# Attention and two feed-forward layers on one core: raw weight words fetched later and rescaled on two engines, and two sum groups moved into the last layer

## The chip, the cores and the metric

The kernel runs on one core of a Trainium2 chip. The metric is the device time of one execution in microseconds; the median of several executions counts. Engines are named as the profile names them: PE (TensorE; PEld are its weight loads), DVE (VectorE), ACT (ScalarE), POOL (GpSimd) and SP (SyncE, which here only issues DMAs; SPq is its queue).

## The reference

```python
def _attn_ref(q, k, v, M_prev, z_prev, beta):        # B, H, S, D = 4, 8, 576, 64
    scores = scale * np.matmul(q, k.transpose(0, 1, 3, 2))      # causal mask, softmax -> a
    local = np.matmul(a, v)
    q_p = phi(q)
    mem_out = einsum('bhsd,bhde->bhse', q_p, M_prev) / (einsum('bhsd,bhd->bhs', q_p, z_prev) + 1e-06)
    return g * mem_out + (1 - g) * local                        # g = sigmoid(beta), per head
def _moe_ref(x, w_in, w_out):                        # 2304 tokens, 512 -> 2048 -> 512
    h = x @ w_in
    return (h * np.cos(h)) @ w_out
def _moe2_ref(x, w_in, w_out):
    h = x @ w_in
    return (h * np.tanh(softplus(h))) @ w_out
reference = _moe2_ref(_moe_ref(_attn_ref(...)))
```

The four weight matrices come in as float64 and reach the chip as pairs of 32-bit words; the kernel turns each pair into float32 itself.

## The kernel before

**Stages.** The attention runs over 16 pairs of heads with five steps each (`stage_a`: scores, mask, exp and the row's weighting; `stage_b`: transposes; `stage_c`: the output). The first feed-forward layer is computed in two halves of its 2048 hidden units. The first half (`seq1`, 256 tokens at a time) is woven into the attention from about 120 us on and ends at about 480 us; the second half (`seq2`, 512 tokens at a time) runs from there to about 670 us. The last layer (`strassen_ffn`) does its products with seven sums of blocks in place of eight blocks, in 24 groups of about 14.5 us.

**Raw words.** `fetch` loads 512 KB of raw word pairs into one of four `wst` buffers from SP's queue, and `to_f32` makes float32 of them in four steps: the high word is rescaled (`scaled(kind, ...)`, line 134 on POOL, line 130 on ACT), ACT makes a float of the low word (line 145), and DVE joins the two (lines 146 and 147). For the first layer, `load_half` then splits the result into two parts (`wh`: lines 130 and 134; line 183 subtracts on POOL and DVE in turn); 16 pieces for each half. `TURNS` is a table that says which engine takes each kind of step: `"p"` POOL, `"a"` ACT, `"v"` DVE, several letters in turn.

**Sum groups.** The last layer's weights are 16 pieces (`strassen_pieces`: eight of `w_in`, eight of `w_out`). `strassen_weights` takes two raw loads for each, forms four sums (line 561, POOL), splits seven blocks in four lots (lines 130 and 567) and stores each lot to DRAM (lines 570 and 573, SP's queue), from where `load_w` (line 625) fetches them in the last layer. It is a generator: each `next` is one small step. Six pieces (`gi`) are made during the attention, ten (`gc`) during the second half.

**Order.** A scheduler sets the order on each engine. `tc.issue_after(x)` puts what a block records behind instruction x on x's own engine; it adds no wait for other engines. `marks` holds the latest instruction of a kind: `act` the exp, `vec` the reciprocal of the row sums (line 277), `pool` the weighting of the row (line 279), `sp` the last store of a pair's attention output (line 347).

Of the kernel before, what the change touches and what calls it, by code (L numbers as in the profile page):

```python
# [25 lines left out]
LOAD0 = 9  # L26
AHEAD = 3
SUM0 = 38
SUMS = 6
SUM2 = 2  # L30
XSUM0 = 37
XLOAD0 = 63
CONVR = 0.9
# [4 lines left out]

TURNS = dict(
    sc0="p", aT0="a",  # L40
    sc="p", ws="p", w0l="pv", w1l="vp", w2l="vp", gl="p", gh="v", bh="a", mh="a",
    wh="ap", aT="av", yl="p", ml="p", y0="v", y1="a", aD="v", y3="a", yf="vp", yz="v", mz="vp", x3l="v", x3l0="pv", x3d0="p", x3d="v", ws4="p", ws2="a", wh2="a",
)

# [6 lines left out]
def attention_moe_moe_kernel(  # L51
# [489 lines left out]
                 for tl in range(n)] +  # L541
                [([wo[:, f] for f in (2 * tl, 2 * tl + 1)], "h c f", woD[tl]) for tl in range(n)])

    def strassen_weights(pieces):

        made = []
        raws = ahead([src for srcs, _, _ in pieces for src in srcs])
        for _ in range(AHEAD):
            next(raws)
            yield  # L550
        for _, order, dst in pieces:
            pc = []
            for _ in range(2):
                pc.append(next(raws).rearrange(f"p ({order}) -> p h c f", c=2, h=2))
                yield
            (a11, a21), (a12, a22) = [[q[:, h] for h in range(2)] for q in pc]
            sw = wk.tile([P, 4, 2, P], F32, tag="sw", name="sw", bufs=BUFS["sw"])
            s1, s2, s3, s4 = [sw[:, k] for k in range(4)]
            for i, (d, x, y, op) in enumerate(((s1, a21, a22, ALU.add), (s2, s1, a11, ALU.subtract),
                                               (s3, a11, a21, ALU.subtract), (s4, a12, s2, ALU.subtract))):  # L560
                turn_of("ws4").tensor_tensor(d, x, y, op)
                if i % 2:
                    yield
            for k0, k1, t in ((0, 2, pc[1]), (2, 3, pc[0][:, 0:1]), (3, 5, sw[:, :2]), (5, 7, sw[:, 2:])):
                ws = wk.tile([P, 2, 2, 2, P], F32R, tag="ws", name="ws", bufs=BUFS["ws"])[:, :k1 - k0]
                scaled("wh2", ws[:, :, 0], t)
                turn_of("w2l").tensor_tensor(ws[:, :, 1], t, ws[:, :, 0].bitcast(F32), ALU.subtract)
                made.append((dst[:, k0:k1], ws.rearrange("p k l c f -> p k (l c f)").bitcast(F32)))
                if len(made) > 1:
                    nc.sync.dma_start(*made.pop(0))  # L570
                yield
        for m in made:
            nc.sync.dma_start(*m)

    def strassen_x(t0, out, store=False):

# [63 lines left out]
                es.enter_context(tc.issue_after(marks[e]))  # L640
        return es

    def strassen_ffn(pool, xs, w, fill):

        ng = DFF // (2 * P)
        groups = [(t0, tl) for t0 in range(0, NT, 2 * TS) for tl in range(ng)]
# [5 lines left out]
        stores = []  # L652
        chain = [(k, name) for k in range(0, n, KS) for name in LAST]
        g3 = [wk.tile([P, 2, TS], F32R, tag=f"g3{i}", name="g3", bufs=1) for i in range(BUFS["g3"])]
        sums = [wk.tile([P, TS], F32, tag=f"ac{i}", name="ac", bufs=1) for i in range(14)]
        free = list(range(BUFS["g3"]))

        def bank():
# [109 lines left out]
        for k in range(n + KS):  # L768
# [4 lines left out]
            def product(b, name, first):  # L773
                m = 0
                for c in range(2):
                    for wl, xl in ((0, 0), (0, 1), (1, 0)):
                        nc.tensor.matmul(b, w[name][:, wl, c], x[name][:, xl, c], start=first and m == 0, stop=m == 5,  # L777
                                         skip_group_check=True)
                        m += 1
                if k + 1 < n:  # L780
                    nw[name] = load_w(groups[k + 1][1], name)
                j = PROD.index(name)
                for a in range(STEPS.count((groups[k][1] - ng, j))):
                    with behind():
                        next(coming, None)
# [72 lines left out]
    k_done = 0  # L858
    pieces = [-AHEAD]
    pieces2 = strassen_pieces(w2i, w2o)  # L860
    gi = strassen_weights(pieces2[:SUMS])

    def converted(n):
        while pieces[0] < min(n, 4 * NTL):
# [2 lines left out]

    for kind, s in at:
        if kind == "a" and s >= LOAD0:
            converted(min(s - LOAD0 + 1 - AHEAD, 0))  # L870
        if kind == "a" and s >= CONV0:
            with tc.issue_after(marks["act"]):
                converted(int((s - CONV0 + 1) * CONVR))
        if kind == "a" and s >= SUM0 - AHEAD:
            with tc.issue_after(marks["act"]), tc.issue_after(marks["pool"]), tc.issue_after(marks["vec"]):
                for _ in range(2 if s % 5 == 0 else 1):
                    next(gi, None)
        if kind != "c":
            continue
        b, r = divmod(s, steps_b)  # L880
        if r == steps_b - 1:
            stored[0] = b + 1
        if b == 0:
            continue
        share = (r + 1) / steps_b
        tgt = int(2 * NTL * (b - 1 + (share ** PACE1 if b == 1 else share))) - RES
        while k_done < tgt:
            converted(4 * min(k_done + 2, NTL))
            _, kk = next(m1)
            k_done = max(k_done, kk + 1)  # L890
# [7 lines left out]
                    done_b = next(gb, done_b)  # L898
    b_pools = [psum("psB")]
    drain(gi)  # L900
    gc = strassen_weights(pieces2[SUMS:])
    fill = []
    m2 = ffn(b_pools, seq2, {1: w_b}, elem_cos("bh"), load_block(xsH, xsL, True), mm2_t, fin_full, tail=fill)
    gx = strassen_x(0, {}, True)
# [27 lines left out]
    with tc.issue_after(last_sin[0]):  # L932
        table = nc.scalar.preload_act_table_set("mish").ins
    with tc.issue_after(table), tc.issue_after(marks["xs"]):
        drain(strassen_ffn(b_pools[0], xs, w0, fill))


_OUTS = [((512, 2304), "float32")]
# [62 lines left out]
```

## Time and profile before

| | us |
|---|---|
| median of 3 runs | 1048.62 (1046.93 to 1053.64) |
| the profiled execution's own time | 1047.3 |
| its span, first to last instruction | 1045.5 |
| PE busy in the span | 1006.4 (96%) |
| DVE, ACT, POOL busy | 680.9, 576.8, 625.8 |

PE is busy nearly all the time, so the table is read by its gaps: 39 us of the span in which PE does nothing, and stretches in which its granted clock is below 1.00.

### The profile page before, as it was taken

The numbers are of one execution on the slowest core, as the hardware profiler recorded it, in microseconds if no ns is written. First come the engines' busy times: TensorE is split into PE (matmuls) and PEld (weight loads), VectorE is DVE, ScalarE is ACT, GpSimd is POOL, SyncE is SP. The second block draws the span as 40 slices with busy tenths as digits, with TensorE's granted clock in tenths as the row PEclk, the third lists the DMA queues.
The fourth block names the chain that finished last, engine by engine and source line by source line (L and its number), as shares of the span: only waits on it lengthen the run. The fifth ranks groups of instructions, "written<-read, shape, count | busy, mean of one in ns | idle before, by whom it ended". The sixth has DMA issues, their size and how long they took to land.

```text
span 1045.5 us, 19409 instructions
## 1 busy us (share of the span) xinstructions
PE 1006.4 (96%) x6704; PEld 895.4 (86%) x6704; DVE 680.9 (65%) x1411; ACT 576.8 (55%) x1274; POOL 625.8 (60%) x612
## 2 busy tenths in 40 slices
PE   6988999999999999999999999999999999999996
PEld 3755788787878899998887777999999999999996
DVE  4689865657665545787775877252788347862657
ACT  5886776758575643334565646345453544445441
POOL 3379744455554524655766788355778767786662
PEclk8998999999999999999999999999999999999999
DMA  7477634546442437433788888987987888797882
GB/s 266 136 238 241 208 128 161 180 159 224 151 146 80 145 105 258 151 101 131 264 287 277 327 295 321 402 306 226 321 271 252 276 285 292 235 311 236 276 285 81
DMA packets 121841, 236.19 MB, mean 226 GB/s; under 512 B 11920, under 2 KB 35984, under 8 KB 121744
## 3 DMA queue, kind: packets, MB, share of 16 engines
q1 hardware_dynamic: 121744, 234.95, 66.2%
q8 instruction: 54, 0.88, 0.4%
q14 instruction: 43, 0.35, 0.1%
HBM read 176.44 MB, written 58.46 MB: 225 GB/s over the span
## 4 chain that ended last, share of the span: by engine, by line
PE 76%; DMA 7%; DVE 6%; ACT 3%; POOL 3%; issue 3%; SPq 1%; DVEq 0%; POOLq 0%; ACTq 0%
PE y L494 16%; PE h L777 15%; PE h L428 15%; PE y L748 15%; PE o L339 4%; PE tp L312 3%; PE sp L252 3%; PE o L328 1%; PE mp L292 1%; DMA qd<-in_qT_dram 1%; DMA wst<-in_w1o_dram 1%; DMA xbH<-xsH 1%; POOL at L279 1%; DMA w<-woD 1%; ACT u L387 1%
## 5 line engine op out<-in xcount | busy, mean ns | idle before, releaser
L682 POOL TENSOR_TENSOR g<-us,g 128x384 fp32r<-128x384 f32 x164 | 180.3, 1117 | 99.6 <-ACT g L130 96.3
L494 PE MATMUL y<-g,w 128*128 128x256 f32 (+1 forms) x1344 | 222.8, 318 | 7.1 <-POOL g L400 3.6
L494 PEld LDWEIGHTS y<-g,w 128*128 128x128 f32 x1344 | 191.5, 190 | 35.0 <-issue 10.5
L428 PE MATMUL h<-xbH,w 128*128 128x256 f32 (+1 forms) x896 | 206.5, 317 | 1.3 <-DMA xbH<-xsH 1.3
L748 PE MATMUL y<-g,w 128*128 128x384 f32 x1008 | 195.3, 335 | 3.0 <-DMA w<-woD 2.2
L777 PE MATMUL h<-xc,wq 128*128 128x384 f32 x1008 | 195.5, 334 | 0.0
L748 PEld LDWEIGHTS y<-g,w 128*128 128x128 f32 x1008 | 176.0, 188 | 5.1 <-DMA w<-woD 2.6
L777 PEld LDWEIGHTS h<-xc,wq 128*128 128x128 f32 x1008 | 176.1, 188 | 0.2 <-DVE us L671 0.2
L279 POOL TENSOR_SCALAR at<-at,sm,omg 128x128 f32<-128x128 f32 (+2 forms) x144 | 113.5, 798 | 103.3 <-DVE sm L277 85.8
L400 POOL TENSOR_TENSOR g<-u,g 128x512 fp32r<-128x512 f32 x72 | 103.1, 1449 | 112.5 <-ACT g L130 47.4
L428 PEld LDWEIGHTS h<-xbH,w 128*128 128x128 f32 x896 | 150.9, 191 | 14.4 <-DMA xbH<-xsH 2.1
L428 PE MATMUL h<-xbL,w 128*128 128x256 f32 (+1 forms) x448 | 140.7, 314 | 0.0
L671 DVE TENSOR_TENSOR us<-h,us 128x384 f32<-128x384 f32 x120 | 66.4, 554 | 113.2 <-PE h L777 97.4
L130 ACT ACTIVATE g<-us 128x384 fp32r<-128x384 f32 x168 | 85.7, 523 | 53.9 <-DVE us L666 33.8
L675 ACT ACTIVATE us<-us 128x384 f32<-128x384 f32 x72 | 37.7, 524 | 94.9 <-DVE us L671 94.2
L428 PEld LDWEIGHTS h<-xbL,w 128*128 128x128 f32 x448 | 85.6, 191 | 5.2 <-issue 0.2
L257 ACT ACTIVATE at<-at,mn 128x128 f32<-128x128 f32 (+3 forms) x128 | 70.9, 555 | 25.3 <-DVE mn L254 24.6
L382 ACT ACTIVATE u<-h 128x512 int32<-128x512 f32 x72 | 41.9, 590 | 67.2 <-PE h L428 66.2
L147 DVE SCALAR_TENSOR_TENSOR wst<-wst 128x512 int32<-128x512 int32 x64 | 73.8, 1165 | 0.3
L712 DVE TENSOR_TENSOR ac<-y,ac 128x384 f32<-128x384 f32 x120 | 63.5, 549 | 14.5 <-PE y L748 14.0
L312 PE MATMUL tp<-ident,at 128*128 128x128 f32 x384 | 63.4, 284 | 8.3 <-POOL at L279 5.3
L390 DVE TENSOR_TENSOR u<-h,u 128x512 f32<-128x512 f32 x72 | 46.3, 685 | 36.4 <-ACT u L387 36.4
(106 smaller groups left out, 1538.6 us busy)
## 6 DMA issues: line engine op xcount, KB each, us to landing
wq<-wsD SPq DMA_DIRECT2D x168, 256.0 KB, 3.9
w<-woD SPq DMA_DIRECT2D x168, 256.0 KB, 4.3
wsD<-ws SPq DMA_DIRECT2D x24, 512.0 KB, 3.8
woD<-ws SPq DMA_DIRECT2D x24, 512.0 KB, 5.6
wst<-in_w1i_dram SPq DMA_DIRECT2D x16, 512.0 KB, 4.4
wst<-in_w1o_dram SPq DMA_DIRECT2D x16, 512.0 KB, 4.8
wst<-in_w2i_dram SPq DMA_DIRECT2D x16, 512.0 KB, 4.3
wst<-in_w2o_dram SPq DMA_DIRECT2D x16, 512.0 KB, 5.7
```

The costliest lines, as they stand in the source:

```text
L130: eng.activation(dst, src, AF.Copy, scale=scale)
L147: nc.vector.scalar_tensor_tensor(lo, hi, 3, lo, ALU.logical_shift_left, ALU.bitwise_or)
L257: marks["act"] = nc.scalar.activation(at[:, :N], at[:, :N], AF.Exp, bias=mn[:, j:j + 1], scale=-1.0, accum_out=sm[:, j:j + 1]).ins
L279: marks["pool"] = turn_of("sc", b == 0).tensor_scalar(at[:, :N], at[:, :N], sm[:, j:j + 1], gates[j], ALU.mult, ALU.mult).ins
L312: nc.tensor.transpose(tp[:, c:c + P], at[:, c:c + P], ident)
L400: marks["gl"] = turn_of(kind).tensor_tensor(gL, g, gH.bitcast(F32), ALU.subtract).ins
L428: nc.tensor.matmul(h[:, a * T:(a + 1) * T], w_[:, c, f0:f0 + P], x_[c], start=m == 0, stop=m == 3 * NC - 1)
L494: nc.tensor.matmul(y[e // per][:, cols], w_[:, f, es], g_, start=fst and m == 0 and e % per == 0, stop=lst and m == 2, skip_group_check=True)
L671: marks['v'] = nc.vector.tensor_tensor(c, b, x, ALU.add).ins
L682: ins = turn_of("ml" if k + 1 < n else "mz").tensor_tensor(t[:, 1], x, t[:, 0].bitcast(F32), ALU.subtract).ins
L748: nc.tensor.matmul(y, w_[:, wl, c], x[:, xl], start=m == 0, stop=m == 3 * KS - 1, skip_group_check=True)
L777: nc.tensor.matmul(b, w[name][:, wl, c], x[name][:, xl, c], start=first and m == 0, stop=m == 5, skip_group_check=True)
```

## The change

1. `ws="pa"`: the rescaling of the first layer's raw high words goes to POOL and ACT in turn; it was on POOL alone.
2. The first raw loads (`LOAD0`) are put behind `marks["sp"]`, the first pair's store, on SP's queue. The conversion steps from `CONV0` on are put behind the attention step's exp, its weighting on POOL and its reciprocal on DVE; they were put behind the exp alone.
3. Two of the sixteen pieces (`LATE`, the last two of `w_out`) leave `gc` and are made in the last layer, by `late` steps behind five of the seven products of each group from the second group on. `SUM2` is 5 in place of 2, so that the second half takes 1.2 steps for each unit in place of 1.5.
4. The stores of the pieces in `gc` and of the two late ones are issued from ACT's queue; `gi` stays on SP's.
5. The fourteen accumulators of the last layer are slices of one tile.

```diff
-SUM2 = 2
+SUM2 = 5
+LATE = 2
-    sc="p", ws="p", w0l="pv", ...
+    sc="p", ws="pa", w0l="pv", ...
-    def strassen_weights(pieces):
+    def strassen_weights(pieces, queue):
-                    nc.sync.dma_start(*made.pop(0))
+                    queue.dma_start(*made.pop(0))
-            nc.sync.dma_start(*m)
+            queue.dma_start(*m)
-    def strassen_ffn(pool, xs, w, fill):
+    def strassen_ffn(pool, xs, w, fill, late):
-        sums = [wk.tile([P, TS], F32, tag=f"ac{i}", name="ac", bufs=1) for i in range(14)]
+        sums = wk.tile([P, 14, TS], F32, name="ac")
+        sums = [sums[:, i] for i in range(14)]
...
                 j = PROD.index(name)
+                if k >= 1 and j not in (0, 3):
+                    with behind():
+                        next(late, None)
...
-    gi = strassen_weights(pieces2[:SUMS])
+    gi = strassen_weights(pieces2[:SUMS], nc.sync)
...
         if kind == "a" and s >= LOAD0:
-            converted(min(s - LOAD0 + 1 - AHEAD, 0))
+            with tc.issue_after(marks["sp"]):
+                converted(min(s - LOAD0 + 1 - AHEAD, 0))
         if kind == "a" and s >= CONV0:
-            with tc.issue_after(marks["act"]):
+            with tc.issue_after(marks["act"]), tc.issue_after(marks["pool"]), tc.issue_after(marks["vec"]):
                 converted(int((s - CONV0 + 1) * CONVR))
...
-    gc = strassen_weights(pieces2[SUMS:])
+    gc = strassen_weights(pieces2[SUMS:-LATE], nc.scalar)
+    gd = strassen_weights(pieces2[-LATE:], nc.scalar)
...
-        drain(strassen_ffn(b_pools[0], xs, w0, fill))
+        drain(strassen_ffn(b_pools[0], xs, w0, fill, gd))
```

In the built program, SP's queue begins as follows before the change (`qd`, `kd`, `qt`, `mz` and `vt` are the attention's inputs of a pair, `wst` the raw words):

```order
L220 DMA qd<-in_qT_dram 128x640
L218 DMA kd<-in_kT_dram 128x576
L104 DMA gate<-in_beta_dram 128x8
L229 DMA qt<-in_qp_dram 128x576
L138 DMA wst<-in_w1i_dram 128x2x512
L223 DMA mz<-in_mbd_dram 128x130
L138 DMA wst<-in_w1i_dram 128x2x512
L138 DMA wst<-in_w1o_dram 128x1024
L226 DMA vt<-in_vn_dram 128x640
```

After it, the same four raw loads stand on SP's queue behind the first pair's two stores:

```order
L227 DMA vt<-in_vn_dram 128x640
L347 DMA xsH<-xH 128x576
L348 DMA xsL<-xL 128x576
L139 DMA wst<-in_w1i_dram 128x2x512 x2
L139 DMA wst<-in_w1o_dram 128x1024 x2
L221 DMA qd<-in_qT_dram 128x640
```

All four raw loads have moved past the inputs of the first four pairs.

On POOL, in the attention's fifth pair, before the change (`at` is the weighting, `wst` the rescaling, `w_101` and its like the split of the finished words):

```order
L134 TENSOR_SCALAR wst<-wst 128x512
L183 TENSOR_TENSOR w_101<-wst,w_100 128x512
L134 TENSOR_SCALAR w_100<-wst 128x512
L279 TENSOR_SCALAR at<-at,sm,omg 128x384 x2
L134 TENSOR_SCALAR wst<-wst 128x512 x2
L279 TENSOR_SCALAR at<-at,sm,omg 128x512 x2
L134 TENSOR_SCALAR wst<-wst 128x512
L183 TENSOR_TENSOR w_103<-wst,w_102 128x512
L279 TENSOR_SCALAR at<-at,sm,omg_123 128x576
```

After it, on POOL, in the same steps of the attention:

```order
L280 TENSOR_SCALAR at<-at,sm,omg 128x384 x2
L135 TENSOR_SCALAR w_100<-wst 128x512
L280 TENSOR_SCALAR at<-at,sm,omg 128x512
L184 TENSOR_TENSOR w_101<-wst,w_100 128x512
L280 TENSOR_SCALAR at<-at,sm,omg 128x512
L135 TENSOR_SCALAR wst<-wst 128x512
L280 TENSOR_SCALAR at<-at,sm,omg_123 128x576
L184 TENSOR_TENSOR w_103<-wst,w_102 128x512
```

Of four rescalings one is left in this stretch, and it stands behind the weighting of its step.

On ACT, in the second half, before the change (`h` to `u` and `g` belong to the layer itself, `ws` and `wst` to the sum groups):

```order
L130 ACTIVATE ws<-wst 128x2x256
L130 ACTIVATE ws<-wst 128x256
L130 ACTIVATE g<-u 128x512 x2
L382 ACTIVATE u<-h 128x512
L130 ACTIVATE ws<-sw 128x2x256
```

After it, on ACT, at the same place of a piece:

```order
L131 ACTIVATE ws<-wst 128x2x256
L131 ACTIVATE ws<-wst 128x256
L131 ACTIVATE wst<-wst 128x512
L146 ACTIVATE wst<-wst 128x512
L571 DMA woD<-ws 128x1024
L131 ACTIVATE g<-u 128x512 x2
L571 DMA woD<-ws 128x1024
L131 ACTIVATE ws<-sw 128x2x256
L383 ACTIVATE u<-h 128x512
```

The stores stand between the layer's own operations; ACT's queue holds 40 of them (32 in the second half, 8 in the last layer), and SP's queue keeps 24 of its 64.

## Rows read from the trace of the kernel before

**Rows 1.** The page, part 1: busy us (share) x instructions of each engine.

```profile
PE 1006.4 (96%) x6704; PEld 895.4 (86%) x6704; DVE 680.9 (65%) x1411; ACT 576.8 (55%) x1274; POOL 625.8 (60%) x612
```

**Rows 2.** Windows: us; PE, PEld, DVE, ACT, POOL busy; clock; DMA share; GB/s.

```profile
0.00:28.00 28.00, 18.65 (x89) 11.34 (x90) 12.66 (x56) 16.87 (x50) 10.44 (x25) 0.88 0.71 250
8.00:16.00 8.00, 5.18 (x24) 2.47 (x20) 4.43 (x17) 6.32 (x22) 5.27 (x10) 1.00 1.04 403
16.00:24.00 8.00, 5.95 (x26) 3.83 (x26) 3.46 (x13) 4.83 (x13) 2.06 (x3) 0.57 0.73 254
60.00:124.00 64.00, 53.52 (x403) 38.96 (x401) 58.84 (x169) 46.49 (x138) 58.53 (x59) 0.92 0.70 224
418.00:523.00 105.00, 105.00 (x703) 97.32 (x702) 81.62 (x96) 46.22 (x73) 64.45 (x54) 1.00 0.48 163
523.00:660.00 137.00, 130.82 (x579) 106.65 (x578) 95.81 (x113) 78.98 (x132) 99.67 (x82) 1.00 0.86 306
672.00:760.00 88.00, 87.98 (x539) 87.67 (x538) 43.25 (x69) 44.47 (x89) 51.59 (x48) 1.00 0.85 294
```

**Rows 3.** Waits of PE, 0 to 28 us: us in total, times, longest.

```profile
PE sp L252 <- DMA kd<-in_kT_dram: 4.5, 1, 4.5
```

**Rows 4.** Timeline of SP's queue: the first of four raw loads.

```profile
2.59 0.43 SPq L138 DMA_DIRECT2D wst<-in_w1i_dram  x1
```

**Rows 5.** Groups, 60 to 124 us: count | busy, mean ns | idle before, releasers.

```profile
L146 DVE SCALAR_TENSOR_TENSOR wst<-wst 128x512 int32<-128x512 int32 x15 | 14.3, 953 | 3.1 <-POOL wst L134 3.1
...
L147 DVE SCALAR_TENSOR_TENSOR wst<-wst 128x512 int32<-128x512 int32 x15 | 12.7, 845 | 0.0
...
L134 POOL TENSOR_SCALAR wst<-wst 128x512 f32<-128x512 f32 x12 | 11.0, 915 | 4.9 <-DMA wst<-in_w1o_dram 3.9 <-DMA wst<-in_w1i_dram 0.9
...
L145 ACT ACTIVATE wst<-wst 128x512 int32<-128x512 uint32 x14 | 9.5, 680 | 3.5 <-DMA wst<-in_w1o_dram 2.7 <-DMA wst<-in_w1i_dram 0.8
```

**Rows 6.** Waits of PE, 60 to 124 us.

```profile
PE tp L312 <- POOL at L279: 5.3, 2, 3.3
PE o L328 <- DVE mo L297: 3.7, 1, 3.7
```

**Rows 7.** Timelines of DVE and POOL: start, us, instruction, idle before.

```profile
69.51 1.47 DVE L146 SCALAR_TENSOR_TENSOR wst<-wst 128x512 int32<-128x512 int32 x1
83.68 0.68 DVE L146 SCALAR_TENSOR_TENSOR wst<-wst 128x512 int32<-128x512 int32 x1
113.43 0.67 POOL L134 TENSOR_SCALAR wst<-wst 128x512 f32<-128x512 f32 x1 [2.53 <-DMA wst<-in_w1o_dram]
```

**Rows 8.** Waits of PE, 523 to 660 us.

```profile
PE y L494 <- POOL g L400: 3.6, 3, 1.7
...
PE h L428 <- DMA xbH<-xsH: 1.3, 2, 0.7
```

**Rows 9.** Waits of SP's queue, whole span.

```profile
SPq L570 <- POOL ws L567: 63.3, 23, 8.2
...
SPq L570 <- DVE ws L567: 37.6, 21, 7.5
```

**Rows 10.** Groups of the whole span: the sum groups' operations.

```profile
L147 DVE SCALAR_TENSOR_TENSOR wst<-wst 128x512 int32<-128x512 int32 x64 | 73.8, 1165 | 0.3
...
L561 POOL TENSOR_TENSOR sw<-wst 128x256 f32<-128x256 f32 x32 | 30.7, 970 | 3.7 <-issue 1.4 <-POOL g L400 1.4 <-POOL ws L567 0.7
...
L567 POOL TENSOR_TENSOR ws<-sw,ws 128x512 fp32r<-128x512 f32 x16 | 22.1, 1380 | 1.8 <-ACT ws L130 1.8
...
L567 DVE TENSOR_TENSOR ws<-wst,ws 128x512 fp32r<-128x512 f32 x16 | 15.6, 976 | 1.1 <-ACT ws L130 0.6
```

**Rows 11.** DMA issues: count, KB each, median us to landing.

```profile
woD<-ws SPq DMA_DIRECT2D x24, 512.0 KB, 5.6
...
wst<-in_w2o_dram SPq DMA_DIRECT2D x16, 512.0 KB, 5.7
```

**Rows 12.** Waits of PE, 660 to 1020 us.

```profile
PE y L748 <- DMA w<-woD: 2.2, 2, 1.7
```

More of the change, by code (lines that the diff above doesn't have):

```diff
@@ L40 @@
     sc0="p", aT0="a",
-    sc="p", ws="p", w0l="pv", w1l="vp", w2l="vp", gl="p", gh="v", bh="a", mh="a",
+    sc="p", ws="pa", w0l="pv", w1l="vp", w2l="vp", gl="p", gh="v", bh="a", mh="a",
     wh="ap", aT="av", yl="p", ml="p", y0="v", y1="a", aD="v", y3="a", yf="vp", yz="v", mz="vp", x3l="v", x3l0="pv", x3d0="p", x3d="v", ws4="p", ws2="a", wh2="a",
```

## The prediction

> **What bounds the kernel now.** I read the page's first part, then windows of busy time by stage, then the waits of PE inside the stages, and last the groups and queues that the change moves. The page shows PE busy 1006.4 us of the 1045.5 us span [rows 1]. The change takes no matmul away, so all that it can win is PE's idle time (39.1 us) and what the lowered clock costs. The windows show where these lie [rows 2]. From 0 to 28 us PE is idle for 28 - 18.65 = 9.35 us, 4.5 of them before its first input has landed [rows 3]; from 16 to 24 us the granted clock is 0.57, between the levels 1.2 and 2.4 GHz, after the idle pieces just before, and costs (1 - 0.57) x 8 = 3.4 us of full-speed work. From 60 to 124 us, where the first layer's raw words are converted beside the attention, PE is idle for 10.5 us and the clock of 0.92 costs another 5.1. From 418 to 523 us PE has no gap at all. From 523 to 660 us, where ten pieces of sum groups are made beside the second half, it is idle for 137 - 130.82 = 6.2 us, and from 672 to 760 us, the first groups of the last layer, for nothing [rows 2]. So the ceiling is 4.85 + 3.4 at the start, 15.6 in the conversion and 6.2 in the second half, some 30 us, and the only place to lose much is a stretch that is full now.
>
> **Late raw loads (the start).** Four loads of 512 KB leave the first 10 us, the first of them issued at 2.59 us [rows 4]. From 8 to 16 us the DMA engines are full (share 1.04 at 403 GB/s) [rows 2]; 2.1 MB at that rate are 5.2 us of their time, and the inputs of the next pairs stood behind them. They go to the place behind the first pair's store, still ahead of the conversion, which lies from 60 us on [rows 5], so the delay itself I cost at nothing; if that cover is gone, POOL's waits for raw words in that stretch, 3.9 + 0.9 us now [rows 5], come a second time. Four rescalings of 0.7 us leave POOL's queue there as well. The gain lies between 0 (the first pairs are a chain through DVE and ACT that no load shortens) and the ceiling of 8.2. I take 3: less than half, since only a part of PE's waits here goes back to a load.
>
> **Conversion behind the weighting, on two engines (60 to 124 us).** PE waits 5.3 us for a weighting on POOL and 3.7 us for `mo` on DVE [rows 6]. Both engines are nearly full: POOL 58.5 and DVE 58.8 of 64 us, ACT 46.5 [rows 2]. Twelve rescalings of 915 ns are in the window, and DVE's joins waited 3.1 us for them [rows 5]. After the change sixteen raw pieces lie in this stretch (four came from the start), eight on POOL and eight on ACT: POOL sheds 4 x 0.915 = 3.7 us, ACT takes 8 x 0.68 = 5.4 us at the price of its low-word step (680 ns) [rows 5], and goes to 51.9 of 64. The weighting now stands ahead of the step's conversion on POOL, so the wait of 5.3 us should mostly go. But DVE keeps every join and every split, and it has only 64 - 58.84 = 5.2 us left. With DVE in that state the stretch can't shrink by much more than those 5.2 us, whatever the ceiling of 15.6 says. I take 4.5, close to DVE's idle time. The ends: a rescaling that waits for its raw load now holds ACT in place of POOL (one such wait took 2.53 us on POOL [rows 7]), with the exp and the copies of transposes queued behind it; ACT's waits for raw words, 3.5 us now [rows 5], could double, which makes -3.5. If DVE's own contention falls too, it is 9. The raw words of the second half of the layer change engines in the same way between about 385 and 560 us; PE waits for nothing there (418 to 523 us), and ACT has 105 - 46 = 59 us free for its share, so I cost that at nothing; without that room it would be 8 x 0.68 = 5.4 us.
>
> Two joins of the same shape took 1.47 and 0.68 us, and only POOL's work beside them differs [rows 7]. The Trainium skill (SBUF — State Buffer, Who interferes with whom) says that a DVE instruction with two inputs in SBUF and a GpSimd instruction that reads SBUF exclude each other for the whole instruction. By that rule DVE's time would fall with POOL's; the third rival below is this mechanism, with a price from rows.
>
> **Fewer sums, and their stores on ACT's queue (523 to 660 us).** Two of ten pieces leave and the step rate falls from 1.5 to 1.2 for each unit, a fifth of the sum groups' work. PE's waits there are for POOL's split of `g` (3.6 us) and for loads [rows 8]. POOL is busy 99.7 of 137 us [rows 2]; a fifth less of sums makes the first kind rarer. SP's queue loses 32 stores here, on which it stood 63.3 + 37.6 = 100.9 us in 44 waits, 2.3 us each [rows 9], with the loads of `xb` and `yp` queued behind. Of the 6.2 us I take 3 back, and 5 as the upper end. What is added: 32 stores on ACT, some 0.43 us of issue each (as on SP [rows 4]), 13.8 us, and each waits for POOL's or DVE's split. Behind it on ACT stand the layer's conversion of `h`, the sine and the split of `g`, for which PE waits in the end. ACT has 137 - 79 = 58 us free, so the issue is covered; the waits are the second rival. Lower end -5.
>
> The queue itself should bring no bandwidth, and rows can't show that it would: all DMAs of this trace come from one engine. The Trainium skill (DMA: Bandwidth & Descriptors, Issuing engines are not separate DMA queues) says that DMAs of all issuing engines run on the same 16 DMA engines and that a second issuer saves only issue time. By that sentence alone the queue's change is worth nothing here and the gain is a fifth of 6.2, or 1.2 us; that is the fourth rival.
>
> **Two pieces in the last layer (about 690 to 760 us).** Each piece costs POOL 4 x 0.97 + 1.38 + about 0.9 = 6.2 us, DVE two times 0.9 + 1.17 and two splits of about 0.98, 6.1 us [rows 5, 10], and ACT eight steps of at most 0.68, 5.4 us, and four stores. Two pieces: 12 us on each. From 672 to 760 us POOL has 36, DVE 45 and ACT 44 us free, and PE no gap [rows 2], so the work is covered unless it falls between a product and the sum that the next product waits for. The DMAs: 2 MB of raw loads and 3.7 MB of stores [rows 11] in some 72 us are 79 GB/s on top of 294 at a share of 0.85, which makes 1.08: full. PE waited for a load of weights twice in this layer, 2.2 us together [rows 12]. I take -1; the lower end is what doesn't fit, 0.08 x 72 = 5.8 us. That the accumulators are one tile makes the first write wait for all that lay in the room before; once, and covered like the rest: 0.
>
> **The sum.** 3 + 4.5 + 3 - 1 = 9.5 us less. Span 1045.5 - 9.5 = 1036.0; the profiled execution took 1047.3, 1.8 more than its span, so 1037.8, which I give as 1037.5. That execution stands 1.3 us below the median of 1048.62. About 1%, 10.5 us, is what a measurement here can tell from no change: the three runs lie 6.7 us apart.
>
> **Rivals.**
> 1. DVE holds the conversion stretch where it is, and the waits for POOL only become waits for DVE: 4.5 becomes 0, and 1042. For: 58.8 of 64 us busy, and its work unchanged. Against: 3.1 us of its idle time were waits for POOL's rescaling.
> 2. Slower: ACT's queue. A store on ACT holds all behind it until POOL or DVE has made its lot. With 58 - 13.8 = 44 us left, ACT is the bound from a mean wait of 44/32 = 1.4 us on. At SP's 2.3 us it is short by 32 x 2.3 - 44 = 29 us: 1037.8 + 3 + 29 = 1070. For: those waits on SP. Against: SP had nothing else to do while it stood there, and on ACT most stores stand several instructions behind the lot that they store, by which time it is made.
> 3. Less of POOL makes DVE itself faster. 953 and 845 ns against 0.68: 15 x 0.27 + 15 x 0.17 = 6.6 us of the joins are lost to contention; a rescaling gone gives back up to 0.68, four 2.7: 1035.
> 4. The stores' queue is worth nothing: 1.2 in place of 3, 1039.6.
> 5. The waits all go, as nothing but the order was at fault: 7 at the start, 13 in the conversion, 5 in the second half: 1047.3 - 25 = 1022. Against: DVE.
> 6. The last layer's DMAs overflow: -5.8 in place of -1, 1042.6. Against: 1.04 was reached in other places without a wait of PE.
>
> That the change doesn't do what it says is excluded by the order: the loads, the stores and the rescalings are where the edits put them.
>
> **How the numbers follow.** Chances: the forecast 0.38, rivals 1 to 6: 0.16, 0.07, 0.10, 0.10, 0.10, 0.09. A time below 1038.1 is faster by over 1%: half the forecast and small parts of 1, 4 and 6 (0.22), rivals 3 and 5 (0.19): 0.41, and with the upper ends together I say 0.43. Above 1059 lies only rival 2: 0.07. The rest is 0.50. The range from 1025 to 1050 leaves out rival 2 and the far part of 5, and takes in all ends of single terms; a loss in ACT of half its price is out as well.
>
> **What would show it.** Clock near 1 from 16 to 24 us; PE's waits on `at` from 60 to 124 us gone, and DVE still near 59 us in that stretch; PE's waits for `g` below 2 us in the second half; no idle of PE from 672 to 760 us. Wrong would make it: ACT idle in front of its stores with PE waiting for `g`, or a new wait for `us` or for weights in the last layer.

## The result and the profile after

The changed kernel takes 1056.7 us in the median of 20 runs (1049.1 to 1060.33), the kernel before 1048.2 in as many beside them: a ratio of 1.0076, with a 95% interval of 1.0061 to 1.0090. It is slower by 0.8% where the forecast was 1% faster. The profiled execution took 1055.44 us, its span is 1053.7.

Part 1 of the page after, which answers to [rows 1]:

```profile
PE 1013.7 (96%) x6704; PEld 899.0 (85%) x6704; DVE 670.9 (64%) x1411; ACT 585.0 (56%) x1290; POOL 613.9 (58%) x596
```

PE's idle time is 1053.7 - 1013.7 = 40.0 us, 0.9 more than before. PE is busy 7.3 us longer with the same 6704 matmuls. So most of the loss isn't idle time at all. Windows of the kernel after say what it is (columns as in [rows 2]):

```profile
0.00:28.00 28.00, 18.31 (x88) 11.74 (x90) 10.19 (x49) 15.29 (x42) 7.21 (x19) 0.88 0.53 177
16.00:26.00 10.00, 7.51 (x34) 4.93 (x35) 3.25 (x14) 5.55 (x17) 2.35 (x3) 0.66 0.17 43
60.00:124.00 64.00, 52.97 (x408) 37.37 (x408) 56.82 (x169) 52.04 (x149) 47.43 (x52) 0.92 0.69 226
106.00:118.00 12.00, 12.00 (x81) 8.89 (x77) 9.04 (x28) 7.23 (x23) 6.73 (x7) 0.57 0.55 189
146.00:154.00 8.00, 7.46 (x40) 5.00 (x40) 5.07 (x21) 5.22 (x16) 2.81 (x4) 0.57 0.46 154
328.00:332.00 4.00, 4.00 (x23) 4.00 (x23) 1.69 (x9) 3.72 (x12) 3.78 (x5) 0.57 0.15 56
418.00:523.00 105.00, 105.00 (x747) 99.24 (x746) 77.98 (x98) 49.18 (x78) 55.81 (x45) 1.00 0.42 135
523.00:660.00 137.00, 136.88 (x608) 113.11 (x607) 90.83 (x107) 76.17 (x124) 91.71 (x73) 1.00 0.81 286
672.00:760.00 88.00, 85.08 (x538) 84.08 (x537) 49.31 (x73) 50.19 (x102) 58.47 (x54) 1.00 0.95 340
```

What a stretch below full speed costs is its length times the missing clock. From 18 to 24 us the granted clock is 0.50, the lower of its two levels, 1.2 and 2.4 GHz; 0.57 and 0.66 are means over such stretches with their edges. There are four: (1 - 0.66) x 10 = 3.4 us from 16 us, 5.2 from 106, 3.4 from 146 and 1.7 from 328, together 13.7. Before, it was 3.4 from 16 us and 1.7 three times between 76 and 122 us: 8.5. These 5.2 us are in PE's busy time. The second half has lost its idle time (0.1 of 137 us, before 6.2), and the last layer, which had none from 672 to 760 us, now has 2.9. Of the signs that the prediction named, PE's waits for `g` went; the clock near 1 from 16 to 24 us and the end of the waits for weightings did not come; and a sign of being wrong came, a new wait for `us`.

The table puts the loss on stages, in us of the profiled executions. Its points are the starts of three stores of attention output on SP (`xsH`; the first, sixth and sixteenth pair), of the last product of the first layer and of the last product of the last one. The experiments that it shows are told below.

| | store 1 | store 6 | store 16 | first layer's end | last layer's end |
|---|---|---|---|---|---|
| before | 34.5 | 126.8 | 385.1 | 696.2 | 1038.0 |
| after | 37.7 | 129.3 | 396.3 | 700.2 | 1046.2 |
| after - before, per stage | +3.2 | -0.7 | +8.8 | -7.2 | +4.2 |
| e1: turns and order | 33.4 | 121.6 | 381.5 | 688.4 | 1029.1 |
| e9: the same, with late pieces, stores on SP | 33.3 | 120.6 | 380.4 | 684.3 | 1026.2 |
| e14: e9 with late loads | 38.3 | 127.7 | 394.4 | 698.8 | 1039.2 |
| e10: e9 with stores on ACT | 32.9 | 120.2 | 379.9 | 682.4 | 1029.9 |

Waits of PE in three stretches of the kernel after, 0 to 28 us, 60 to 124 us and 660 to 1020 us (us in total, times, longest):

```profile
PE o L329 <- DVE den L297: 4.8, 1, 4.8
```

```profile
PE tp L313 <- POOL at L280: 3.6, 3, 2.7
PE o L329 <- DVE aD L133: 3.2, 1, 3.2
```

```profile
PE h L779 <- ACT us L797: 2.6, 1, 2.6
```

Before, the waits from 0 to 28 us were, beside the one of [rows 3]:

```profile
PE tp L312 <- DVE mn L254: 1.5, 3, 0.8
PE o L328 <- DVE den L295: 1.4, 1, 1.4
PE o L339 <- ACT aT L130: 1.0, 1, 1.0
PE mp L292 <- DVE ph L233: 0.9, 1, 0.9
```

So the wait for `den` at the start was 1.4. The reason of its growth stands on DVE's timeline after:

```profile
12.48 0.69 DVE L255 CUSTOM_DVE_ANT_0 at<-sp,mask 128x512 f32<-128x512 f32 x1
...
16.12 0.76 DVE L234 SCALAR_TENSOR_TENSOR ph<-qt,ph 128x576 f32<-128x576 f32 x1 [2.94 <-ACT ph L233]
16.79 0.16 DVE L278 RECIPROCAL sm<-sm 128x2 f32<-128x2 f32 x1
16.87 0.14 DVE L296 SCALAR_TENSOR_TENSOR den<-mp,igate 128x6 f32<-128x6 f32 x1
```

`ph` is the second pair's; `den` is the first pair's, and PE waits for it. Before, `den` came first. With the raw loads out of the way the scheduler put the second pair's `qt`, and with it `ph`, ahead.

The largest loss, 8.8 us between store 6 and store 16, has no term in the prediction. ACT's timeline where the first unit of the first layer meets the attention:

```profile
139.33 0.60 ACT L131 ACTIVATE aT<-tp 128x512 f32<-128x512 f32 x1 [2.33 <-DMA xsL<-xL]
139.94 1.28 ACT L388 ACT_TABLE_LOAD   x1
141.24 1.15 ACT L388 ACTIVATE u<-u,c_hpi 128x1024 f32<-128x1024 f32 x1
142.29 0.67 ACT L232 ACTIVATE ph<-qt 128x576 f32<-128x576 f32 x1
142.98 1.28 ACT L233 ACT_TABLE_LOAD   x1
144.27 0.68 ACT L233 ACTIVATE ph<-ph 128x576 f32<-128x576 f32 x1
...
145.02 0.59 ACT L131 ACTIVATE aT<-tp 128x512 f32<-128x512 f32 x1
```

A copy of transposes waits 2.3 us for the store of an `xL` with which it shares nothing but a place in memory: in the built program this `aT` and that `xL` start at the same address, and the copy waits for the counter of that store. Behind it stand the sine, two table loads and the next pair's `ph`, and then the second copy, for which PE waits 1.6 us. PE's idle pieces here are followed by the stretch from 146 us at 0.57. From 124 to 250 us PE is idle for 4.0 us, before for 0.9; with the clock from 146 and 328 us (3.4 + 1.7) that is 8.2 of the 8.8.

In the last layer, ACT's timeline around PE's wait of 2.6 us (ACTq rows are DMA issues):

```profile
750.89 0.33 ACTq L571 DMA_DIRECT2D woD<-ws  x1
751.27 0.53 ACT L677 ACTIVATE us<-us 128x384 f32<-128x384 f32 x1 [4.18 <-DMA w<-woD]
...
757.61 0.33 ACTq L574 DMA_DIRECT2D woD<-ws  x1
757.98 0.52 ACT L131 ACTIVATE g<-us 128x384 fp32r<-128x384 f32 x1 [3.72 <-DMA woD<-ws]
758.41 0.47 ACT L797 ACTIVATE us<-h 128x384 f32<-128x384 f32 x1
```

Two stores hold ACT for 4.2 and 3.7 us, and the last thing that ended is a DMA each time. POOL had made their lots at 749.3 and 754.7 us (line 568 on its timeline), 1.6 and 2.9 us before the stores went out. In the built program each of the two waits for a DMA counter beside the engine that made the lot:

```
L571 DMA woD<-ws 128x512 [waits DMAHW7_49,Pool_49]
...
L574 DMA woD<-ws 128x1024 [waits DMAHW0_49,Pool_49]
```

There are eight such counters, and the loads on SP wait and count on the same ones. In the built program the first of the two stores waits in this way for a load of weights on SP's queue, the second for the store that ACT itself issued at 751.35 us. So a store on ACT waits for an earlier transfer as well as for its lot, and `x1`, the copy for which PE waits (line 797), stands behind it.

### The profile page after: what moved, and what is told of

The parts are those of the page before. It is cut to its first block, busy times and chain, and to the rows that moved or that the text cites. A ratio compares the mean times of both kernels' runs of the same rounds, so it can differ in the third digit from the quotient of the medians.

```text
span 1053.7 us, 19294 instructions
## 1 busy us (share of the span) xinstructions
PE 1013.7 (96%) x6704; PEld 899.0 (85%) x6704; DVE 670.9 (64%) x1411; ACT 585.0 (56%) x1290; POOL 613.9 (58%) x596
## 5 line engine op out<-in xcount | busy, mean ns | idle before, releaser
L401 POOL TENSOR_TENSOR g<-u,g 128x512 fp32r<-128x512 f32 x72 | 105.4, 1478 | 124.5 <-DVE g L133 44.6
L677 ACT ACTIVATE us<-us 128x384 f32<-128x384 f32 x72 | 37.7, 524 | 93.3 <-DVE us L673 89.1
L384 DVE SCALAR_TENSOR_TENSOR u<-u,h 128x512 f32<-128x512 int32 x72 | 48.8, 681 | 47.6 <-ACT u L383 41.8
L313 PE MATMUL tp<-ident,at 128*128 128x128 f32 x384 | 65.8, 290 | 7.6 <-POOL at L280 3.6
L255 DVE CUSTOM_DVE_ANT_0 at<-sp,mask 128x128 f32<-128x128 f32 (+3 forms) x128 | 59.1, 483 | 21.0 <-PE sp L253 12.8
```

The costliest lines, as they stand in the source:

```text
L313: nc.tensor.transpose(tp[:, c:c + P], at[:, c:c + P], ident)
L401: marks["gl"] = turn_of(kind).tensor_tensor(gL, g, gH.bitcast(F32), ALU.subtract).ins
```

## The experiments

Theory A: the loss is in the attention, from the late loads. Theory D: the stores on ACT cost the last layer. Rivals are named in the expectations. Where an experiment gives up a buffer to make room, its expectation says so.

**e12, one tile alone.** The term that was costed at nothing.

```diff
-        sums = [wk.tile([P, TS], F32, tag=f"ac{i}", name="ac", bufs=1) for i in range(14)]
+        sums = wk.tile([P, 14, TS], F32, name="ac")
+        sums = [sums[:, i] for i in range(14)]
```

> Before, with one edit: the fourteen accumulators as slices of one tile. The prediction's term is 0: ratio 0.999 to 1.001. If the first write's wait or the other places in memory cost something, above 1.002.

1047.3 us, ratio 0.9996 (0.9983 to 1.0008). It costs nothing that can be measured; runs with and without it can be compared.

**e8, the order of the conversion alone.**

```diff
-            with tc.issue_after(marks["act"]):
+            with tc.issue_after(marks["act"]), tc.issue_after(marks["pool"]), tc.issue_after(marks["vec"]):
```

> Before, with one edit: the conversion behind exp, weighting and reciprocal; the rescaling stays on POOL. Together with the turns this gave 0.9912. If the order does it (PE's waits of 5.3 us for weightings on POOL go, and with them lowered clock): 0.991 to 0.994. If the turns do it (POOL sheds 3.7 us in the stretch): 0.998 to 1.000.

1048.16 us, 1.0006 (0.9988 to 1.0024). The order alone is worth nothing, although PE's wait for weightings on POOL from 60 to 124 us falls from 5.3 to 0.2 us. The turns alone were not tried, so whether they need the order is open.

**e1, order and turns.** The same with `ws="pa"`.

> Before, with parts of the attention's change alone: the rescaling in turn, and the conversion behind exp, weighting and reciprocal; the raw loads are not put behind the first store, the sums and their queue stay as before. Theory A (the loss comes from the order in the attention: PE's wait of 4.8 us for den at the start, because the late loads let the next pair's ph go ahead of it, 3 us; and the conversion, squeezed into 60 to 155 us by the late loads, with two more windows at the lower clock, 5 us): without the late loads both go, 1045 to 1050. Rival B (the loss comes from the late pieces in the last layer, 4 to 8 us, and the attention's lag is made up later): 1043 to 1048 here too, the attention being harmless. Rival C (the turns and the order of the conversion alone cost it, since the rescaling on ACT stands ahead of its copies): 1053 to 1057.

1038.37 us, 0.9912 (0.9896 to 0.9927), 9 us gained, more than either theory had. Rival C falls. The sixth store comes 5.2 us earlier and the sixteenth 3.6; the rest comes in the second half (4.2) and the last layer (1.1).

**e2, all of the attention's edits.** e1 with the late loads and the one tile.

```diff
-            converted(min(s - LOAD0 + 1 - AHEAD, 0))
+            with tc.issue_after(marks["sp"]):
+                converted(min(s - LOAD0 + 1 - AHEAD, 0))
```

> All three edits of the attention (late loads, turns, conversion behind the weighting) and the one tile of accumulators; the sums and their queue stay as before. Theory A: the attention loses 9 us and the second half regains nothing: 1055 to 1061, with a clock of 0.98 to 0.987. Rival B (the loss is in the last layer): 1046 to 1050. Rival C (turns and order alone): as A.

1049.22 us, 1.0023 (1.0007 to 1.0038). This lies in B's range and below A's (from 1055): the late loads take back all that e1 gained, but not all of the loss is here.

**e4, late loads without turns and order.** The changed kernel with `ws="p"` and the conversion behind the exp alone.

> The changed kernel with the rescaling on POOL alone and the conversion behind the exp alone, as before the change; the late loads stay. Theory A: the start keeps its 3 us, the conversion loses what the late loads cost it: 1050 to 1057, with PE waiting for den at the start 4 to 5 us. Rival C (turns and order alone): the loss goes, 1044 to 1049, and PE waits from 60 to 155 us as before.

1050.24 us, 1.0032 (1.0019 to 1.0045), with PE's wait for `den` of 4.3 us: at the lower edge of A's range. Turns and order, worth 9 us in e1, cost 4.5 when they are added to this kernel (1.0076): the same two edits have either sign, depending on where the loads are. And without them the late loads cost little: the sixteenth store stands at 388.5 us, 3.4 later than before and 1 later than in e12, where it stands at 387.5.

**e3, all stores on SP.** The changed kernel with `nc.sync` for `gc` and `gd`.

> The changed kernel with the stores back on SP's queue, two pieces still late. If the queue gives the second half its 5 us, PE's waits for g and xb come back there and this takes 1059 to 1062; if fewer sums alone do it, it takes 1056 to 1058, as the changed kernel. If the stores on ACT cost the last layer (PE's wait of 2.6 us for us on ACT), 1053 to 1055.

1048.53 us, 1.0010 (0.9991 to 1.0029): faster than the change by some 7 us, more than any of the three readings allowed. The second half takes 304.1 us from store 16 on, in the changed kernel 303.9: the queue is worth nothing there, and fewer sums do it.

**e5, only the late stores back on SP.** `nc.sync` for `gd`.

> The changed kernel with the eight stores of the two late pieces back on SP's queue; the 32 of the second half stay on ACT's. With all 40 on SP it took 0.7% less than with all on ACT (1.0010 against 1.0076 of before). Theory D (a store on ACT in the last layer holds the Mish and the copies behind it, ACT stood 4.2 and 3.7 us there and PE 2.6): the eight are all of it, ratio 1.000 to 1.002, and PE's wait for us at 759 us goes. Rival E (the 32 stores of the second half shift what follows): 1.006 to 1.008 as the changed kernel.

1052.67 us, 1.0035 (1.0018 to 1.0052). PE's wait for `us` is gone, but the time stands between e3 and the changed kernel: by the ratios the eight stores cost 4.3 us of the 6.9, as D has it. The other 2.6, E's, are no larger than the intervals of e3 and e5 (e11 asks again).

**e6, `ph` behind `den`.** e3, and in `prep` for the second pair:

```diff
+            with tc.issue_after(marks["mo"]) if (b, p) == pairs[1] else ExitStack():
                 nc.vector.scalar_tensor_tensor(ph, qt, 0.0, ph, ALU.max, ALU.add)
```

> The changed kernel with all stores on SP (which gave 1.0010 of before), and the second pair's ph on DVE ordered behind the first pair's den and mo; one buffer fewer for the last layer's wq, which makes room. Theory A: PE's wait for den at the start (4.2 us) falls to about 1.4, the first store stands at 34 instead of 38.4 us, the kernel gains 3 to 4.5 us: ratio 0.9965 to 0.998. Rival F (the late loads lose their time in the conversion alone, the start is made up): 1.001.

1049.31 us, 1.0000 (0.9982 to 1.0019). PE's wait for `den` fell from 4.2 to 1.4 as expected, the first store came only 1.1 us earlier, and against e3 the kernel gained 0.0010, within the intervals of both. A's mechanism at the start, though it is there, isn't the price of the late loads.

**e7, without the late loads, with fewer sums.** e1 with parts 3 and 5 of the change, and `kd=3`.

> The turns and the order of the conversion without the late loads (0.9912 of before alone), with two late pieces, all stores on SP, and one tile of accumulators; one buffer fewer for kd, which makes room. If fewer sums are worth the 6 us that the second half lost between two of the runs, and the last layer covers them: 0.985 to 0.988. If they only move the attention's weaving, 0.990 to 0.995.

1043.28 us, 0.9947 (0.9936 to 0.9959): a miss of the first reading. The buffer is to blame: e9, which gives up another one, is 9 us faster. Its first store stands at 39.9 us, and this window of it at a clock of 0.66, 6.8 us lost:

```profile
14.00:34.00 20.00, 17.98 (x75) 11.79 (x75) 9.35 (x40) 11.80 (x34) 3.69 (x7) 0.66 0.37 133
```

**e9, the same with another buffer given up.** `g3=16` in place of `kd=3`.

> The turns and the order of the conversion without the late loads (0.9912 of before alone), with two late pieces, one tile of accumulators, all stores on SP; one buffer fewer for the last layer's g3 makes room, and the attention's order on PE and ACT is that of the run that gave 0.9912. From the profiles: attention 381.5 us as there, second half 304 us as in every kernel with fewer sums (307 there), last layer 340.5 as with all stores on SP: a span of 1034 less 1 to 3, ratio 0.986 to 0.989. Rival: the sums move the attention's waits by where the tiles lie in memory: 0.990 to 0.995.

1034.25 us, 0.9869 (0.9850 to 0.9888), the best of all: 1.3% faster than before and 2% faster than the change. The second half takes 304 us as expected, the last layer 341.9 with the late pieces in it (before 341.8): when SP stores them they are covered, to a us or so.

**e10, e9 with all 40 stores on ACT.**

> The same with all 40 stores on ACT's queue, as the change has them; the attention is the same word for word. Theory D (a store on ACT in the last layer waits for its own place in the row of earlier transfers and holds Mish and the copies behind it): 4 to 7 us more than with the stores on SP, all of it after 660 us, and PE waits for us on ACT. Rival: the queue was no cause, the difference between the two earlier runs was the attention's: within 1 us of the run before.

1042.35 us, 0.9945 (0.9925 to 0.9966). The queue costs 8.1 us by the medians; the profiled run, the fastest of this kernel (1039.2), shows 4.2 of it after store 16. The six executions go from 1039.2 us at a mean clock of 0.991 to 1044.78 at 0.987, so part of the rest goes with the clock; where it falls, no profile shows. Where the cost shows, windows and ACT's timeline agree with the changed kernel; 700 to 760 us of e10:

```profile
700.00:760.00 60.00, 56.77 (x324) 55.69 (x323) 38.30 (x59) 33.26 (x70) 52.91 (x48) 1.00 0.94 330
```

and of e9:

```profile
700.00:760.00 60.00, 59.33 (x342) 59.01 (x342) 43.76 (x61) 34.40 (x72) 55.01 (x49) 1.00 0.96 341
```

and on ACT in e10:

```profile
735.42 0.53 ACT L677 ACTIVATE us<-us 128x384 f32<-128x384 f32 x1 [6.20 <-DMA xr<-ysF]
...
741.94 0.52 ACT L131 ACTIVATE g<-us 128x384 fp32r<-128x384 f32 x1 [3.67 <-DMA wq<-wsD]
```

PE is idle 3.2 us there against 0.7. The last thing to end ahead of the two stores is a transfer (`xr`, `wq`) that has nothing to do with them; POOL had made their lots 3.6 and 2.7 us earlier.

**e11, e9 with the 32 stores of the second half on ACT.**

> The same with the 32 stores of the second half on ACT and the eight of the last layer on SP. Theory D: as with all stores on SP, within 1.5 us. If the 32 stores cost as well: between the two runs before it. In the second half all three take 303.5 to 304.5 us, since the queue is worth nothing there.

1038.03 us, 0.9908 (0.9892 to 0.9924): 3.8 us over e9. The eight late stores cost 4.3, the 32 others 3.8, which D didn't have and E did. The second half itself is not longer by more than 0.3 us; where the 3.8 lie, the profile, with 1.8 more from store 16 to the end, doesn't settle.

**e14, e9 with the late loads.** The clean pair to e9: one edit, all else the same.

> The best run so far (0.9869) with one edit: the first raw loads behind the first pair's store, as the change has them. Everything else, buffers too, is the same. If the late loads are the cause of the loss in the attention: 0.998 to 1.003, all of it before 400 us.

1049.12 us, 1.0019 (1.0002 to 1.0035). The late loads cost 14.9 us by the medians. The spans of the two profiled executions lie 12.9 us apart, and in the table the sixteenth store comes 14.0 later. Windows of e14:

```profile
0.00:420.00 420.00, 392.80 (x3163) 313.26 (x3164) 262.71 (x827) 275.60 (x718) 200.89 (x241) 0.97 0.53 175
14.00:26.00 12.00, 7.37 (x32) 4.63 (x32) 3.25 (x14) 7.15 (x21) 2.45 (x4) 0.57 0.22 69
98.00:110.00 12.00, 9.61 (x75) 7.86 (x75) 11.19 (x33) 7.94 (x20) 8.33 (x12) 0.72 0.75 255
144.00:156.00 12.00, 11.15 (x56) 8.05 (x57) 7.21 (x23) 6.26 (x19) 4.63 (x6) 0.57 0.31 102
```

and of e9:

```profile
0.00:420.00 420.00, 401.73 (x3280) 324.67 (x3281) 274.15 (x841) 282.58 (x730) 207.68 (x245) 0.98 0.53 179
14.00:22.00 8.00, 6.42 (x24) 3.88 (x24) 4.19 (x15) 5.85 (x16) 2.19 (x4) 0.57 0.96 362
78.00:90.00 12.00, 11.31 (x64) 8.08 (x65) 10.29 (x29) 8.00 (x25) 8.96 (x9) 0.57 0.67 219
146.00:154.00 8.00, 8.00 (x65) 6.36 (x64) 6.00 (x21) 7.78 (x17) 4.58 (x5) 1.00 0.24 72
```

The lowered clock costs 5.2 + 3.4 + 5.2 = 13.8 us in e14, 3.4 + 5.2 = 8.6 in e9. The stretch at 144 us, with the wait of a copy for an `xL` store as in the changed kernel (2.7 us), is the difference. PE's idle time up to 420 us is 27.2 us in e14 and 18.3 in e9: 8.9 more, and with the 5.2 of the clock that is the 14. It lies in three places: 2.9 up to 60 us, where the wait for `den` is 4.5 us; 2.9 from 60 to 124, where PE waits 3.6 us for weightings on POOL and in e9 not at all; 3.2 from 124 to 250, where the copy waits. With its clock the last of the three is the largest, 8.4 us.

**e13, the loads in between.** e9 with the raw loads behind the third pair's `qt`, at 17.7 us, ahead of the first store and with `den` ahead of `ph`; `xr=3`.

> The best run so far (0.9869: turns, order, two late pieces, all stores on SP) with the first raw loads ordered behind the third pair's qt on SP, so between 18 and 30 us instead of at 10 us, and still ahead of the first store; one buffer fewer for the last layer's xr makes room. The order on DVE keeps den ahead of the second pair's ph. Theory A' (the late loads cost their 13 us because the order of the first three pairs changes once the loads are gone from the start): 0.986 to 0.990, as if they had not moved. Rival G (any delay of the raw words costs, since the conversion and the next pairs' inputs come later): 0.993 to 1.001.

1042.73 us, 0.9958 (0.9945 to 0.9972). A' falls: 8.5 us are lost by the medians although the loads are only 8 us later than in e9, the order of `ph` and `den` is e9's and the clock is better (0.993 against 0.989 in the profiled runs). G is shown in part only. The profiled runs lie 4.6 us apart, 3.0 of them at the sixteenth store and 1.5 in the last layer, for whose `xr` a buffer was given up, and e7 shows that a buffer can cost 9. PE's wait for weightings from 60 to 124 us is back here too (3.3 us). The scores on PE show a part, groups of 0 to 420 us of e9:

```profile
L253 PE MATMUL sp<-kd,qd 64*128 64x128 f32 (+3 forms) x256 | 63.1, 496 | 4.8 <-DMA kd<-in_kT_dram 4.5 <-DVE mn L255 0.2
```

and of e13:

```profile
L253 PE MATMUL sp<-kd,qd 64*128 64x512 f32 (+3 forms) x256 | 66.6, 493 | 5.7 <-DMA kd<-in_kT_dram 4.5 <-DVE mo L298 0.9 <-DVE xL L345 0.2
```

The same 256 score matmuls take PE 3.5 us more. In e9 twelve of them stand in one row at 23.60 us; with later loads they stand in pieces between transposes and outputs. But the scores take 66.3 us in e4 as well, where the late loads cost little.

## Why the prediction was wrong

**Late raw loads.** This is the step that failed: "the delay itself I cost at nothing", with the conversion's start at 60 us as the cover, and a gain of 3 for the freed DMA engines. With it failed the adding up, which took the conversion's gain to be the same wherever the loads stand. The cover held, as ACT's and POOL's waits for raw words didn't grow (in the changed kernel one of 1.1 us on ACT). The 3 us had no wait behind them: of PE's waits from 0 to 28 us before, only that for `kd`, the very first input, is for a load. What moved was the order. Taking four loads, four rescalings and their times out of the start let the scheduler place the next pairs' inputs, `ph` and scores earlier and in pieces. Measured cost: 14.9 us in the clean pair (e9, e14), 10.9 in e1 and e2, and about 14 between e10 and the changed kernel, which differ in one buffer beside it. That is the price beside the turns and the order. Without these, e4's ratio of 1.0032 leaves the late loads about nothing, as e10 against e1 gives fewer sums and stores on ACT 0.9945 - 0.9912 = 0.0033 (each ratio is sure to 2 us or so). So the late loads cost what the turns and the order had won, and some more; the late loads alone were not run. The diff of the order in front of the prediction showed SP's queue, where the loads moved; that DVE's `ph` had moved ahead of `den` was there to be seen in DVE's order and was not looked for.

Where the cost lies in the profiled pair is shown: 5.2 us are lowered clock and 8.9 idle time of PE. The idle time is about a third each at the start, in the conversion and where the first layer meets the attention, and the 5.2 us stand with the last (e14). Why is settled in part only. At the start it is the wait for `den`, but taking that wait away gained nothing that can be measured (e6), and `den` and scores in pieces stand in e4 too. In the conversion the wait for weightings, which is gone in e1 and e9, is back at 3.5 to 3.6 us in e2, e14 and the changed kernel; what brings it back is not shown, and in e6, with late loads too, it isn't there. Where the first layer begins, the wait of the copy for `xL`'s store was read from the trace: in four profiles where that wait is 2.0 to 2.7 us (the changed kernel, e3, e5, e14) PE waits 1.6 us for the copy and a stretch at lower clock follows; in e6, where it is 0.9, PE waits 0.8 and none follows; in e2 and e4, with late loads too, the copy doesn't wait. It waits because the two tiles share a place in memory, so this part hangs on where the tiles come to lie as well as on the late loads: at the sixteenth store e2, without it, is 8.1 us behind e1, and e14 is 14.0 behind e9. Another place wasn't tried.

**Conversion on two engines behind the weighting.** Taken at 4.5, measured by itself at 9.2 (e1). That this is the far end of its range is luck, since the 9 there was priced by a fall of DVE's contention, which e1 doesn't have (below). The size was right in its own stage: from the first to the sixth store e1 takes 88.2 us, 4.1 less than before. The rest came where no term was: 1.1 before the first store and 5.2 from the sixteenth on, less 1.5 in between. The mechanism is shown in part: the wait for weightings goes, but it goes in e8 too, where nothing is gained, so it takes the turns as well. In the changed kernel the same stage gained 0.7. PE's wait for weightings fell from 5.3 to 3.6 us instead of going, and one for `aD` on DVE took the place of `mo`. The third rival's mechanism is there in the changed kernel: DVE's joins, 60 to 124 us,

```profile
L147 DVE SCALAR_TENSOR_TENSOR wst<-wst 128x512 int32<-128x512 int32 x16 | 12.3, 770 | 1.3 <-POOL wst L135 1.2
L148 DVE SCALAR_TENSOR_TENSOR wst<-wst 128x512 int32<-128x512 int32 x15 | 11.6, 788 | 0.0
```

took 953 and 845 ns before [rows 5]; with POOL busy 47.4 in place of 58.5 us DVE gives back 3.8 us. The Trainium skill's rule (SBUF — State Buffer, Who interferes with whom) agrees with this in direction. But in e1 POOL falls too, to 51.1 us, and the joins stay at 893 and 899 ns, so the 9.2 us came without a faster DVE, and the rival was rightly left out of the sum. The prediction's two joins of 1.47 and 0.68 us don't carry it either: POOL was busy beside both, with a split and a weighting beside the first and a weighting beside the second. In e1 DVE, as busy as before (58.5 of 64 us), didn't hold the stretch, as the first rival would have it.

**Fewer sums.** Taken at 3, upper end 5: 4.5 us by the ratios of e1 and e9 (0.9912 - 0.9869 = 0.0043 of 1047), with the late pieces in it. From store 16 to the first layer's end it depends on the turns: 311.1 us before and 304.0 in e4, without them, but 306.9 in e1 and 304.0 in e9, with them. So the table's 7.2 us there are not all on top of what the turns gain. The mechanism was right and mis-sized: a fifth less of sums freed more than a fifth of the waits, since PE's waits for `g` went altogether ([rows 8]: 3.6 us; now PE is idle 0.1 us there in all).

**The queue.** Taken as part of the 3, with a fall to 1070 as a rival. In the second half it is worth next to nothing (303.9 us with the stores on ACT and 304.1 with them on SP; 302.4 in e10 and 304.0 in e9), which is what the fourth rival and the Trainium skill's sentence (DMA: Bandwidth & Descriptors, Issuing engines are not separate DMA queues) had; the trace agrees within 1.6 us. As a whole it costs 8.1 us (e9, e10): the second rival's mechanism, a store that holds ACT. But the rival was priced by how long POOL or DVE take for the lot, and of the 17.8 us in the four holds shown above 10.8 are the wait for an earlier transfer. The prediction found that the lot is made several instructions ahead and took that as the reason against.

**Late pieces.** Taken at -1: with the stores on SP the last layer takes 341.9 us in e9 and 341.8 before. Over all profiles it takes 338.9 to 341.8 us without late pieces and 339.4 to 343.5 with them on SP, so that 0 and -1 can't be told apart; with the stores on ACT it takes 346.0 to 348.4. The DMA share from 672 to 760 us rises to 0.95, where 1.08 was worked out. The sixth rival, an overflow of the DMA engines, didn't come: PE's waits for weights fell from 2.2 [rows 12] to 0.8 us in the changed kernel and 0.6 in e9. **One tile**: 0, as taken (e12).

So the sum 3 + 4.5 + 3 - 1 should have read, from the runs: late loads -14.9, conversion 9.2, fewer sums with late pieces 4.5, queue -8.1, one tile 0: -9.3, against -8.5 measured. Each of these holds beside the edits that stood with it when it was measured, and e4 shows that elsewhere it can be another.

## What to carry to other kernels

Moving a load that nobody waits for is not free where a scheduler sets the order around it: look at what moves up on every engine into the room that it leaves, and cost that. A DMA issued from a computing engine can wait for other transfers than its own data, and everything behind it on that engine waits too; here the stores did better on a queue that computes nothing. Two gains that are each real need not add up: an edit that was worth 9 us without the late loads cost 4.5 with them (e1, e4). Try each part of a bundle by itself, and then the pairs: without the late loads and the stores on ACT the same bundle was 1.3% faster than before (e9).

## What the runs showed of the hardware

Between the two kernels TensorE's clock decided more than PE's idle time: 5.2 us against 0.9 (in e14 against e9 it was 5.2 and 8.9). In the 20 runs of the changed kernel the mean granted clock lies between 0.979 and 0.992 and the time follows it, from 1060.33 us at 0.980 to 1049.1 at 0.992, though not run for run. Each stretch shown after idle pieces of PE cost 1.7 to 6.8 us more than the idle time itself, so a wait of 1.6 us (up to 145.75 us in the changed kernel, with smaller ones beside it) came to 5.

The same score matmuls on 64 rows take PE less time when many stand in a row, at a granted clock of 1.00 in both kernels. Timeline of PE in e9 (a row merges scores of 256, 384 and 512 columns and names the first):

```profile
23.60 2.21 PE L253 MATMUL sp<-kd,qd 64*128 64x256 f32 x12
```

and in the changed kernel:

```profile
29.19 0.70 PE L253 MATMUL sp<-kd,qd 64*128 64x256 f32 x2
...
31.25 0.70 PE L253 MATMUL sp<-kd,qd 64*128 64x256 f32 x2
...
32.24 1.77 PE L253 MATMUL sp<-kd,qd 64*128 64x384 f32 x8
```

The same twelve take 2.21 us in one row and 3.17 in three pieces. From start to start of what follows it is 2.14 against 2.94 us, so most of the difference isn't overlap of the pieces' ends.
